# Score steps of two units regrouped: seven groups for two units instead of four for one, with PV in the spare PSUM banks

## The chip, the cores and the metric

One core of one Trainium2 chip. The metric is the device time of one execution in microseconds (us). The engines are TensorE (PE, with PEld for its weight loads), VectorE (DVE), ScalarE (ACT), GpSimd (POOL) and SyncE (SP, which here only issues DMAs).

## The reference, cut to what matters

```python
# q, k, v: (8, 12, 448, 64) float32
q_n, k_n = rmsnorm(q, g_q), rmsnorm(k, g_k)
scores = 1/sqrt(64) * q_n @ k_n.T
attn = exp(scores - max) / sum
x = (attn @ v) laid out as (3584, 768)
h = x @ w_in                      # 768 x 2048
out = maximum(0.01*h, h) @ w_out  # 2048 x 768
```

The kernel works in 24 units of four heads (three units to a batch). A unit needs scores in seven steps, exponentials, PV (attn @ v) and the sums z. Every exponential of a unit has one bias, called its shift: VectorE takes the maximum of the unit's step 0 (`shift_max`), a matmul spreads it over the partitions (`shift_mm`, tile `pb`), and VectorE reduces that to the bias `eb`. Until the shift is there, ScalarE can compute no exponential of the unit, and the scores stay in their slots. A slot is a pair of banks of PSUM, the memory that the matmuls here write. When a batch's three units are done, its dense layers go into a queue of items: 6 matmuls of layer 1 (`hps`), or 8 matmuls of layer 2 (`op`). The queue is fed out between the groups of score steps of later units, so that TensorE always has dense work while ScalarE computes exponentials.

## The kernel before

A score step is four matmuls on a quarter of the array each (64x64 tiling). Two score slots of two PSUM banks alternate; four more banks ("spare") serve everything else.

```python
    def slot():
        return psum.tile([P, 2, 512], FP32, tag="sT", bufs=2, name="sT")

    def aux(shape, dtype, name):
        return psum.tile(shape, dtype, tag="aux", bufs=4, name=name)

    def shift_mm(u):                       # after shift_max(u) on VectorE
        ...
        nc.tensor.matmul(pb[:, 0:P], onesp, s["dg"], start=True, stop=True)
        nc.vector.tensor_reduce(s["spare"][:, 510:511], pb[:, 0:P], axis=AXL.X, op=ALU.max)
        s["eb"] = ...                      # bias of every exponential of the unit
        nc.vector.tensor_scalar(s["eb"], s["spare"][:, 510:511], -1.0, DELTA, op0=ALU.mult, op1=ALU.add)

    def pv_slot(u):                        # PV takes a score slot
        s["pslot"] = slot()
        ...
    def pv_out(u):
        nc.scalar.copy(s["x32"], s["pslot"][:, :, 0:S])
    ...
    STEPS = ((0,), (1, 2), (3, 4), (5, 6))
    ...
        for u in range(3, NU):
            for d in range(4):             # four groups for each unit
                ...
                    qk(u, STEPS[d])
                    if d == 0:
                        shift_max(u)
                        if narrow(u - 1):
                            pv_slot(u - 1)
                            zcol(u - 1)
                            shift_mm(u)
                            pv_out(u - 1)
                            zcol_sum(u - 1)
                        ...
                    ex(u)                  # exponentials on ScalarE
                ...
                if d == 1 and u > 3 and narrow(u - 1):
                    xmul_pool(u - 1)       # x = PV * (1/z), on POOL
                ...
                fill(u, d, jobs)           # dense items, with small jobs between them
```

## Time and profile before

| | before |
|---|---|
| first three runs | 437.13 us (437.05 to 437.75) |
| profiled span | 435.7 us |
| TensorE busy | 419.9 us (96%) |
| ScalarE, VectorE busy | 309.9 us (71%), 215.6 us (49%) |
| TensorE waiting for another engine after 98 us | none listed |

TensorE is full, and after 98 us the profile puts nothing in its way. From there on a change pays only if it removes something from TensorE's own stream; whatever makes TensorE wait comes straight on top.

### The profile page before, as it was taken

Reading aid. Unit: us, or ns where it says so; the run is one execution under the profiler, and the core shown is the slowest. Engines: PE = TensorE matmul, PEld = TensorE weight load, DVE = VectorE, ACT = ScalarE, POOL = GpSimd, SP = SyncE. Lnnn points to the kernel's source line nnn. Section 1 sums busy time; section 2 is a strip of 40 time slices with the busy share of each in tenths; the row PEclk is TensorE's granted clock in tenths of the full one; section 3 lists DMA queues with packets and bytes.
Section 4 is the critical chain, followed back from the end, with each engine's and each line's share of the span. In section 5 each row is a group of like instructions: output and inputs, shape, how many; then the busy total and the mean of one; then the engine's idle time right before and its main releaser. Section 6 shows DMA issues by size and latency. Waiting matters only on the chain.

```text
span 435.7 us, 8818 instructions
## 1 busy us (share of the span) xinstructions
PE 419.9 (96%) x3714; PEld 216.9 (50%) x3714; DVE 215.6 (49%) x321; ACT 309.9 (71%) x460; POOL 148.8 (34%) x102
## 2 busy tenths in 40 slices
PE   6878999999999999999999999999999999999995
PEld 6645444444455544554445544554445544555563
DVE  4897565874535744554455745555356611220021
ACT  5989878688976699867876699867877486634300
POOL 4997565633422432532430423522521110100000
PEclk9899999999999999999999999999999999999999
DMA  7999995789458856669447875778524530311022
GB/s 262 248 259 255 238 235 76 195 195 201 96 144 145 215 152 119 136 200 201 91 126 141 200 186 98 154 205 165 125 45 100 132 84 2 78 38 38 0 73 73
DMA packets 66315, 62.37 MB, mean 143 GB/s; under 512 B 35684, under 2 KB 61284, under 8 KB 66276
## 3 DMA queue, kind: packets, MB, share of 16 engines
q1 hardware_dynamic: 55840, 49.82, 44.7%
q0 software_dynamic: 10272, 11.80, 17.4%
q8 instruction: 29, 0.48, 0.4%
q10 hardware_dynamic: 164, 0.20, 0.1%
q14 instruction: 10, 0.08, 0.1%
HBM read 45.61 MB, written 11.01 MB: 130 GB/s over the span
## 4 chain that ended last, share of the span: by engine, by line
PE 84%; ACT 7%; DVE 6%; DMA 2%; issue 1%; SPq 0%; DVEq 0%; ACTq 0%
PE hps L329 33%; PE op L351 31%; PE sT L179 8%; PE sT L314 5%; ACT et L198 3%; PE zc L260 3%; DVE n L151 1%; DMA rk<-in_k_dram 1%; PE pb L228 1%; DVE ssq L139 1%; PE sT L243 1%; PE pv L314 1%; ACT et L196 1%; DVE xt L323 1%; DMA out_dram<-ost 1%
## 5 line engine op out<-in xcount | busy, mean ns | idle before, releaser
L198 ACT ACTIVATE et<-sT,eb 128x896 f16<-128x896 f32 x166 | 158.7, 1004 | 48.0 <-PE sT L179 35.7
L351 PE MATMUL op<-wout,gt 128*128 128x384 f16 x896 | 153.6, 326 | 0.0
L329 PE MATMUL hps<-xt,win 128*128 128x448 f16 x756 | 151.0, 353 | 0.2 <-DVE xt L323 0.2
L351 PEld LDWEIGHTS <-gt 128*128 128x128 f16 x896 | 84.7, 98 | 65.3 <-issue 12.2
L329 PEld LDWEIGHTS <-win 128*128 128x128 f16 x756 | 70.9, 98 | 71.8 <-issue 7.6
L294 POOL TENSOR_TENSOR xt<-x,rz 128x896 f16<-128x896 f32 x19 | 40.9, 2154 | 185.6 <-DMA rz<-zs 170.7
L331 ACT ACTIVATE gt<-hps 128x448 f16<-128x448 f32 x126 | 67.6, 543 | 22.6 <-PE hps L329 21.5
L359 DVE COPY ost<-op 128x384 f32<-128x384 f32 x54 | 30.0, 556 | 94.2 <-PE op L351 90.9
L134 POOL TENSOR_TENSOR qg<-rq,ggb 128x896 f32<-128x896 f32 (+2 forms) x25 | 61.3, 2454 | 36.9 <-DVE n L151 32.6
L179 PE MATMUL sT<-qkT 64*64 64x448 f16 x664 | 52.3, 364 | 4.5 <-ACT et L198 3.8
L151 DVE TENSOR_TENSOR n<-qg,rinv 128x896 f16<-128x896 f32 (+2 forms) x25 | 27.1, 1085 | 54.5 <-POOL xt L294 23.6
L139 DVE TENSOR_REDUCE ssq<-sq 128x14 f32<-128x896 f32 (+2 forms) x49 | 50.0, 1054 | 1.9 <-ACT sq L126 1.9
L216 DVE TENSOR_REDUCE sT<-sT 128x1 f32<-128x896 f32 x22 | 24.1, 1094 | 30.6 <-PE sT L179 30.4
L151 DVE TENSOR_TENSOR n<-rk,rinv 128x896 f16<-128x896 f32 (+2 forms) x25 | 34.2, 1372 | 0.0
L179 PEld LDWEIGHTS <-qkT 64*64 64x64 f16 x672 | 15.2, 104 | 37.9 <-issue 35.4
L272 ACT COPY x<-sT 128x896 f32<-128x896 f32 x19 | 17.2, 905 | 18.0 <-PE sT L314 18.0
L314 PE MATMUL sT<-et,vt 64*64 64x448 f16 x532 | 28.4, 349 | 0.0
L314 PEld LDWEIGHTS <-vt 64*64 64x64 f16 x672 | 19.8, 107 | 10.5
L106 POOL DMA_DIRECT2D vt<-in_v_dram x24 | 18.3, 763 | 0.0
L126 ACT ACTIVATE sq<-rq 128x896 f32<-128x896 f32 (+2 forms) x19 | 17.3, 913 | 1.2 <-DMA rq<-in_q_dram 1.2
L126 ACT ACTIVATE sq<-rk 128x896 f32<-128x896 f32 x17 | 16.2, 955 | 0.7 <-DMA rk<-in_k_dram 0.7
L260 PE MATMUL zc<-et,onesr 128*32 128x448 f16 (+1 forms) x304 | 16.1, 332 | 0.0
(66 smaller groups left out, 216.3 us busy)
## 6 DMA issues: line engine op xcount, KB each, us to landing
rq<-in_q_dram SPq DMA_DIRECT2D x24, 448.0 KB, 4.6
rk<-in_k_dram SPq DMA_DIRECT2D x24, 448.0 KB, 6.1
out_dram<-ost SPq DMA_DIRECT2D x54, 192.0 KB, 3.5
rz<-zs SPq DMA_DIRECT2D x38, 224.0 KB, 3.5
vt<-in_v_dram POOLq DMA_DIRECT2D x24, 224.0 KB, 4.7
win<-in_moe_w_in_dram POOLq DMA_DIRECT2D x8, 384.0 KB, 11.5
wout<-in_moe_w_out_dram POOLq DMA_DIRECT2D x2, 1536.0 KB, 26.9
qkT<-n SPq DMA_TRANSPOSE x18, 4.1
```

The lines of the kernel that those rows point to most:

```text
L126: nc.scalar.activation(buf(u, "sq")[:, ti, :, c[0]:c[1]], raw[u][ti][:, :, c[0]:c[1]], AF.Square)
L134: eng.tensor_tensor(buf(u, "qg")[:, :, c[0]:c[1]], raw[u][0][:, :, c[0]:c[1]], ggb[:, None, None, :].broadcast_to([P, 2, n, D]), op=ALU.mult)
L139: nc.vector.tensor_reduce(buf(u, "ssq")[:, ti, :, c[0]:c[1]], buf(u, "sq")[:, ti, :, c[0]:c[1]], axis=AXL.X, op=ALU.add)
L151: nc.vector.tensor_tensor(buf(u, "n16")[:, ti, c[0]:c[1]].rearrange("p s a d -> p a s d"), src[:, :, c[0]:c[1]], buf(u, "rinv")[:, ti, :, ...
L179: nc.tensor.matmul(banks[a][64 * r:64 * r + 64, 0:S].rearrange("p (t x) -> p t x", t=NS), kT(u, r, a, t), qT(u, r, a), start=True, stop=True)
L198: nc.scalar.activation(s["et"][:, t], sT[:, :, 0:S], AF.Exp, bias=s["eb"], scale=1.0)
L294: nc.gpsimd.tensor_tensor(xts[b][:, g], s["x32"], s["rz"], op=ALU.mult)
L314: nc.tensor.matmul(s["pv"][r][64 * a:64 * a + 64, 0:S], vts[u % NV][64 * r:64 * r + 64, a, t], s["et"][64 * r:64 * r + 64, t, a], start=(t ...
L329: nc.tensor.matmul(hps[:, 0:S], win16[:, kt // 2, kt % 2, ts(ft, P)], xt[:, kt // 2, kt % 2], start=(kt == 0), stop=(kt == KT - 1))
L331: nc.scalar.activation(gt[:, ft, ds(S * (b % 2), S)], hps[:, 0:S], AF.Prelu, bias=0.0, scale=1.0, alpha=0.01)
L351: nc.tensor.matmul(op2[:, 0:HC], gt[:, ft, ts(t, P)], wout16[:, ft, ds(HC * half, HC)], start=(ft == 0), stop=(ft == FT - 1))
L359: nc.vector.tensor_copy(ost[0][:, ds(HC * half, HC)], op2[:, 0:HC])
```

## The change

The intent: fewer, fuller groups. Seven steps don't divide by two, so a unit had one group of one step and three of two. Two units have fourteen steps, seven groups of two (called x0 to x6 below). As x0 and x4 then use both slots for scores, PV moves to two spare banks. Also POOL's multiply for unit 4 is written behind the norms of unit 7. The diff, cut to its core:

```diff
     def pv_out(u):
-        nc.scalar.copy(s["x32"], s["pslot"][:, :, 0:S])
+        ...                                        # still so where PV has a slot
+        for r in range(2):
+            nc.scalar.copy(s["x32"][:, r], s["pv"][r][:, 0:S])
...
+    for u in range(PAIRS, NU, 2):                  # PAIRS = 8
+        order = [(u, t) for t in range(NS)] + [(u + 1, t) for t in range(NS)]
+        for x in range(NS):
+            groups.append((order[2 * x:2 * x + 2], (2.9, 4.0, 4.0, 4.0, 2.9, 4.0, 4.0)[x]))
...
+                elif d == 2:                       # units up to 7: four groups as before
+                    norms(u)
+                    if u == 5:
+                        job(xmul_pool, 4)          # was at d == 1
...
+            if x == 0:
+                shift_max(u)
+                pv(u - 1)                          # spare banks
+                zcol(u - 1)
+                shift_mm(u)
+                pv_out(u - 1)
+                ...
+            elif x == 3:                           # last step of u, step 0 of n = u + 1
+                ex(u)
+                shift_max(n)
+                job(lambda: None)                  # after the first dense item: nothing
+                job(shift_ex, n)                   # after the second: shift_mm(n), ex(n)
+            elif x == 4:                           # begins with steps 1 and 2 of n
+                pv(u)
+                zcol(u)
+                pv_out(u)
+                ...
```

More of the change, by code (lines that the diff above doesn't have):

```diff
@@ L43 @@
     NV = 5
+    PAIRS = 8
     cst = ctx.enter_context(tc.tile_pool(name="cst", bufs=1))
@@ L182, in qk @@
     def qk(u, steps):
-        st[u]["sT"] = []
+        st[u].setdefault("sT", [])
         for t in steps:
@@ L198, in ex @@
                 nc.scalar.activation(s["et"][:, t], sT[:, :, 0:S], AF.Exp, bias=s["eb"], scale=1.0)
+        s["sT"] = []
     def score0(u):
@@ L270, in pv_out @@
         s = st[u]
+        if "pslot" in s:
+            s["x32"] = zpool.tile([P, 2, S], FP32, tag="x32", name="x32")
+            nc.scalar.copy(s["x32"], s["pslot"][:, :, 0:S])
+            return
         s["x32"] = zpool.tile([P, 2, S], FP32, tag="x32", name="x32")
-        nc.scalar.copy(s["x32"], s["pslot"][:, :, 0:S])
+        for r in range(2):
+            nc.scalar.copy(s["x32"][:, r], s["pv"][r][:, 0:S])
     def zcol_sum(u):
@@ L379, in push_moe2, with fed, fill @@
                     queue.append((1.31, lambda b=b, t=t, half=half, part=part: moe2(b // 2, t, half, part)))
-    WD = (3.6, 2.9, 2.8, 2.8)
     STEPS = ((0,), (1, 2), (3, 4), (5, 6))
     debt = [0.0]
+    groups = [((), 3.6)] + [([(3, t) for t in STEPS[d]], 2.9) for d in range(1, 4)]
+    for u in range(4, PAIRS):
+        for d in range(4):
+            groups.append(([(u, t) for t in STEPS[d]], (3.6, 2.9, 2.8, 2.8)[d]))
+    FIRST = len(groups)
+    for u in range(PAIRS, NU, 2):
+        order = [(u, t) for t in range(NS)] + [(u + 1, t) for t in range(NS)]
+        for x in range(NS):
+            groups.append((order[2 * x:2 * x + 2], (2.9, 4.0, 4.0, 4.0, 2.9, 4.0, 4.0)[x]))
     def narrow(u):
         return 4 <= u < NU - 1
-    def fed(u, d):
-        return u % NQ == 0 and d == 3
-    def fill(u, d, jobs):
-        total = sum(c for c, _ in queue)
-        left = WD[d] + 3.0
-        uu, dd = u, d
-        while True:
-            dd += 1
-            if dd == 4:
-                uu, dd = uu + 1, 0
-            if uu == NU or (fed(uu, dd) and (u > 3 or uu > 3)):
+    def fed(gi):
+        if gi < FIRST:
+            u, d = 3 + gi // 4, gi % 4
+            return u // NQ if u > 3 and u % NQ == 0 and d == 3 else 0
+        y, x = divmod(gi - FIRST, NS)
+        u = PAIRS + 2 * y
+        if x == 3 and u % NQ == 0:
+            return u // NQ
+        if x == 0 and (u - 1) % NQ == 0:
+            return (u - 1) // NQ
+        return 0
+    def fill(gi, jobs):
+        total = sum(c for c, _ in queue)
+        w = groups[gi][1]
+        left = w + 3.0
+        for gj in range(gi + 1, len(groups)):
+            if fed(gj) > 0:
                 break
-            left += WD[dd]
-        debt[0] += total * WD[d] / left
+            left += groups[gj][1]
+        debt[0] += total * w / left
         while queue and debt[0] >= queue[0][0] * 0.5:
@@ L595, with early @@
         del queue[0:2]
-        for u in range(3, NU):
-            for d in range(4):
-                if d > 0 or u > 3:
-                    qk(u, STEPS[d])
-                    if d == 0:
-                        shift_max(u)
-                        if narrow(u - 1):
-                            pv_slot(u - 1)
-                            zcol(u - 1)
-                            shift_mm(u)
-                            pv_out(u - 1)
-                            zcol_sum(u - 1)
-                        else:
-                            zsum_slot(u - 1)
-                            pv(u - 1)
-                            shift_mm(u)
-                            zinv(u - 1)
+        def early(u):
+            if u + 4 < NU:
+                job(load, u + 4)
+            if u + 2 < NU:
+                prep_qg(u + 2, nc.gpsimd)
+            if u + 3 < NU:
+                load_v(u + 3)
+            if u < 6:
+                prep_sqp(u + 3)
@@ new lines, in sums_of_squares, with norms, squares @@
+        def sums_of_squares(u):
+            if u + 2 < NU:
+                for ti in range(2):
+                    job(prep_ssq, u + 2, ALL, (ti,))
+        def norms(u):
+            if u + 2 < NU:
+                job(prep_rinv, u + 2)
+                for ti in range(2):
+                    job(prep_norm, u + 2, ALL, (ti,))
+                if u > 3:
+                    job(prep_trd, u + 2)
+        def squares(u, ti):
+            if 6 <= u < NU - 3:
+                job(prep_sq, u + 3, ALL, (ti,))
@@ new lines, in shift_ex, with job @@
+        def shift_ex(u):
+            shift_mm(u)
+            ex(u)
+        for gi, (steps, w) in enumerate(groups):
+            jobs = []
+            def job(fn, *args):
+                jobs.append(lambda: fn(*args))
+            for u, t in steps:
+                qk(u, (t,))
+            if gi < FIRST:
+                u, d = 3 + gi // 4, gi % 4
+                if d == 0 and u > 3:
+                    shift_max(u)
+                    if narrow(u - 1):
+                        pv_slot(u - 1)
+                        zcol(u - 1)
+                        shift_mm(u)
+                        pv_out(u - 1)
+                        zcol_sum(u - 1)
+                    else:
+                        zsum_slot(u - 1)
+                        pv(u - 1)
+                        shift_mm(u)
+                        zinv(u - 1)
+                if gi > 0:
@@ L614 @@
                     ex(u)
-                jobs = []
-                def job(fn, *args):
-                    jobs.append(lambda: fn(*args))
                 if d == 0:
@@ L627 @@
                         xmul(u - 1)
-                    if u + 4 < NU:
-                        job(load, u + 4)
-                    if u + 2 < NU:
-                        prep_qg(u + 2, nc.gpsimd)
-                    if u + 3 < NU:
-                        load_v(u + 3)
-                    if u < 6:
-                        prep_sqp(u + 3)
-                if d == 1 and u > 3 and narrow(u - 1):
-                    xmul_pool(u - 1)
-                if fed(u, d) and u > 3:
-                    push_moe1(u // NQ - 1)
-                    push_moe2(u // NQ - 1)
@@ L641 @@
-                if (u, d) in ((3, 1), (4, 0)):
-                    for ti in range(2):
-                        prep_tr(u + 1, ti, VV)
-                if u + 2 < NU:
-                    if d == 1:
-                        for ti in range(2):
-                            job(prep_ssq, u + 2, ALL, (ti,))
-                    if d == 2:
-                        job(prep_rinv, u + 2)
-                        for ti in range(2):
-                            job(prep_norm, u + 2, ALL, (ti,))
-                        if u > 3:
-                            job(prep_trd, u + 2)
@@ L654 @@
-                if d == 3 and 6 <= u < NU - 3:
-                    for ti in range(2):
-                        job(prep_sq, u + 3, ALL, (ti,))
-                fill(u, d, jobs)
+                    early(u)
+                    if u == 4:
+                        for ti in range(2):
+                            prep_tr(5, ti, VV)
+                elif d == 1:
+                    if u > 3 and u != 5 and narrow(u - 1):
+                        xmul_pool(u - 1)
+                    if u == 3:
+                        for ti in range(2):
+                            prep_tr(4, ti, VV)
+                    sums_of_squares(u)
+                elif d == 2:
+                    norms(u)
+                    if u == 5:
+                        job(xmul_pool, 4)
+                else:
+                    for ti in range(2):
+                        squares(u, ti)
@@ new lines @@
+                if fed(gi) > 0:
+                    push_moe1(fed(gi) - 1)
+                    push_moe2(fed(gi) - 1)
+                fill(gi, jobs)
+                continue
+            y, x = divmod(gi - FIRST, NS)
+            u = PAIRS + 2 * y
+            n = u + 1
+            if x == 0:
+                shift_max(u)
+                pv(u - 1)
+                zcol(u - 1)
+                shift_mm(u)
+                pv_out(u - 1)
+                zcol_sum(u - 1)
+                ex(u)
+                job(zcol_inv, u - 1)
+                early(u)
+                sums_of_squares(u)
+            elif x == 1:
+                ex(u)
+                xmul_pool(u - 1)
+                norms(u)
+            elif x == 2:
+                ex(u)
+                for ti in range(2):
+                    squares(u, ti)
+            elif x == 3:
+                ex(u)
+                shift_max(n)
[5 more added lines that the diff above has]
+                pv_out(u)
+                zcol_sum(u)
+                ex(n)
+                job(zcol_inv, u)
+                early(n)
+                sums_of_squares(n)
+            elif x == 5:
+                ex(n)
+                xmul_pool(u)
+                norms(n)
+            else:
+                ex(n)
+                for ti in range(2):
+                    squares(n, ti)
@@ L658 @@
+            if fed(gi) > 0:
+                push_moe1(fed(gi) - 1)
+                push_moe2(fed(gi) - 1)
+            fill(gi, jobs)
         zsum_slot(NU - 1)
```

## The prediction

> **What bounds the kernel now.** I began with the busy shares, then asked who makes TensorE wait, then read the chain of waits over two units, then one timeline where a wait was left.
>
> ```profile
> PE 419.9 (96%) x3714; PEld 216.9 (50%) x3714; DVE 215.6 (49%) x321; ACT 309.9 (71%) x460; POOL 148.8 (34%) x102
> ...
> PE   6878999999999999999999999999999999999995
> ```
>
> This is the page: TensorE is busy in every slice from the seventh on. ACT averages 71%, and in the stretches that run the first dense layer (160 to 180 us) the windows by 20 us give it 19.0 of 20. The share proves nothing alone, as matmul ends are modelled, so I looked at TensorE's waits.
>
> ```profile
> PE sT L179 <- ACT et L198: 3.8, 9, 0.9
> PE pb L228 <- DVE dg L218: 1.8, 3, 0.8
> ```
>
> Columns: total us, times, longest. Asked by window, both rows are empty after 98 us. So from 98 to 430 us TensorE never waits for another engine; only fewer or cheaper matmul slots can shorten this stretch, and any new wait lengthens it. The chain over one unit shows what its slots cost:
>
> ```profile
> 198.21 4.54 PE hps L329 x24
> 202.75 0.50 PE sT L179 x8
> 203.25 2.38 PE hps L329 x12
> 205.63 0.50 PE sT L179 x8
> 206.13 3.51 PE hps L329 x18
> ...
> 213.65 0.31 PE sT L179 x4
> 213.97 1.32 PE sT L314 x28
> 215.29 0.78 PE zc L260 x16
> 216.07 0.16 PE pb L228
> 216.23 3.40 PE hps L329 x18
> ```
>
> Columns: start, us, what. 18 dense matmuls take 3.40 us when another full-array matmul precedes them (0.189 each) and 3.51 after a score group: 0.11 us for leaving the 64x64 tiling. 28 PV matmuls take 1.32 us, four at a time, so 8 scores should take 0.38 and take 0.50, and 4 should take 0.19 and take 0.31: 0.12 us for entering it. A score group thus costs 0.23 us beyond its work. This is the only waste in the chain that the change can reach after 98 us.
>
> The 0.8 us wait sits here:
>
> ```profile
> 80.52 1.09 DVE L151 TENSOR_TENSOR n<-qg,rinv 128x896 f16<-128x896 f32 x1
> 80.82 2.73 POOL L294 TENSOR_TENSOR xt<-x,rz 128x896 f16<-128x896 f32 x1 [3.95 <-DMA rz<-zs]
> 81.53 2.98 DVE L151 TENSOR_TENSOR n<-rk,rinv 128x896 f16<-128x896 f32 x1
> ...
> 84.90 1.08 DVE L216 TENSOR_REDUCE sT<-sT 128x1 f32<-128x896 f32 x1
> ...
> 86.35 0.22 PE L228 MATMUL pb<-dg,onesp 128*128 128x128 f16 x1 [0.84 <-DVE dg L218]
> ```
>
> In unit 5 the second norm takes 2.98 us where its neighbour takes 1.09, because POOL's multiply for unit 4 runs beside it; DVE then is late for unit 6's maximum and TensorE idles 0.84 us. The multiply itself started at 80.82 because its broadcast 1/z landed then.
>
> **What the Trainium skill says.** "TensorEngine Tiling (Array Packing)", Key Properties: changing the tiling mode drains TensorE. The chain agrees: 0.12 us in, 0.11 us out. "SBUF — State Buffer", Who interferes with whom: a VectorE instruction with two SBUF inputs contends with a GpSimd instruction that reads SBUF. The timeline agrees: 2.98 against 1.09 us. "PSUM — Partial Sum Buffer", Engine vs sequencer instructions: the queues of ScalarE, VectorE and GpSimd are strict FIFO. All my ordering arguments use it; the trace shows nothing against it.
>
> **The change part by part.** I compared the built instruction orders of the two programs.
>
> (1) The multiply moved behind the norms. On POOL the order is unchanged (squares of unit 8, multiply of unit 4, then the next q-times-g), and the multiply waits on the same semaphores with the same values: the two broadcasts and the copy of PV. Writing it later in the source adds no dependency on the norms. So it again starts when the broadcast lands, about 80.8 us, and collides again. Worth: 0; if it worked, 0.84 us.
>
> (2) Units 4 to 7: the same groups. The fill only moves one half-projection (8 matmuls) from group 4 to group 3 of unit 5 and shifts a few later; the TensorE total is equal. Worth: 0.
>
> (3) From unit 8 on, 16 units in 8 pairs. Before, a pair had 8 score groups: 2 of 0.31 and 6 of 0.50, 3.62 us; after, 7 of 0.50, 3.50: 0.12 saved. Returns from a score group straight to dense work: before 6 at 0.11; after 5, plus one from the z sums of the first unit (x4, below), which no longer has a shift matmul behind it. The shift matmuls cost 2 x 0.16 before; after, one 0.16, and one of about 0.05 amid dense matmuls (0.16 less the 0.11 switch). So 0.66 + 0.32 = 0.98 becomes 0.66 + 0.21 = 0.87: 0.11 saved. Together 0.23 per pair, x8 = **1.9 us saved**. PV, z sums and dense matmuls are unchanged in number.
>
> (4) The new wait. Call a pair's seven groups x0 to x6. x3 computes the first unit's last step and the second unit's step 0, then two dense items, the shift matmul, and the rest of its fill. x4 begins with steps 1 and 2 of the second unit. The two score slots alternate, so step 2 needs the slot of step 0, free only after shift, VectorE's bias and the exponential. Before, at a usual boundary: shift 250.15, reduce 250.42, bias 250.75, exponential 250.95 to 251.96. So 1.81 us from the shift's start, plus 0.05 to hand over (67.79 to 67.84 at an early wait) = 1.86. TensorE meanwhile has, by the built order:
> - pairs 8, 14, 20: shift 0.05 + 8 projections 1.30 + step 1 at 0.31 = 1.66; waits 0.2.
> - pairs 12, 18: 0.05 + 6 dense 1.13 + 0.31 = 1.49; waits 0.37. Here an output copy of 0.56 us comes just before the bias in VectorE's queue; I take it to start 0.1 after the shift's start, so the reduce starts near 0.65 instead of 0.27: 0.39 more, 0.76 in all.
> - pairs 10, 16, 22: two dense items, 2.3 us: no wait.
> Sum 3 x 0.2 + 2 x 0.76 = **2.1 us added**. TensorE has no slack elsewhere, so it goes straight into the span.
>
> (5) PV in the spare banks. At x0 two PV banks, the z bank and the shift bank take all four spare banks, so every activation of the group before must be done first; and dense work then waits for ACT to copy PV (now two copies instead of one of 0.91). A ledger for pair 12/14, where six groups of dense layer 1 follow each other, with starts read off ACT at 157 to 166 us (exponential 0.89, activation 0.42, square 0.84 from start to start): from the PV of x4 to the last activation ACT needs some 13.4 us and TensorE reaches the shift after 14.7. It fits by about 1.3 us. I allow **0.3 us** over all eight pairs for cases where it doesn't.
>
> Sum: 437.1 - 1.9 + 2.1 + 0.3 = 437.6. I take **437.4**, leaning a little to the gain, as each wait in (4) depends on tenths.
>
> **Rivals.** (a) The new slot waits do not come, because the profile's 1.81 us contains slack I can't see or ACT is early: then only the switches count, 435.2. For: TensorE never waited for a slot after 98 us before. Against: the slot chain is a plain dependency, and before step 0 had a slot of its own for 5 us. (b) The multiply does move behind the norms in time and the collision goes: another 0.8 less, 434.4 with (a). Against: same queue, same semaphores. (c) ACT becomes the bound in the dense-layer-1 stretches: 95% busy in 160 to 180 us, and PV copies, squares and activations now gate the same four banks. Three boundaries have squares between activations just ahead of PV (units 8, 14, 20); at 0.8 us each, 2.4 more, 440. Against: the ledger above.
>
> **Range and chances.** The best case (a with b) is 434.4, the worst I can build (4 plus c) is 440. The runs before spread over 0.7 us. Eight in ten: 434.6 to 439.6. Two per cent is 8.7 us, over four times the whole saving, and the waits would have to be four times my sum: faster 0.01, within 0.975, slower 0.015.
>
> **What would show it.** TensorE's busy share stays at 95 to 96%. The waits list gains a row of score matmuls waiting for the exponential after 98 us, about 5 times, 2 us in all, the longest near 0.8; in time, only at x4. Each score group stays at 0.50 us and there are 8 fewer of them. The norm of about 3 us at 81 us and the 0.84 us wait of the shift matmul remain. Copies of PV appear as 128x448, 32 of them from unit 7 on. I am wrong if dense matmuls wait for PV copies or activations for more than 1 us in sum, if the shift waits for a bank at units 8, 14 and 20, or if the norm at 81 us drops to about 1.1.

## The result, and the profile after

| | before | after |
|---|---|---|
| median (6 runs each) | 437.44 us (436.85 to 438.05) | 438.17 us (437.45 to 438.49) |
| ratio of fast runs | | 1.0014, 95% interval 1.0001 to 1.0027 |
| profiled span | 435.7 us | 436.4 us |

A ratio is the mean time of one kernel's fast runs over that of the other's in the same rounds, so not quite the ratio of the medians quoted. About 0.15% slower.

Whole times scatter by half a microsecond and more, so I also read stages from the chain of waits. Its PV rows mark the units; a unit's PV stands in the first group of the next unit. First of the kernel before (start, us, what); the marks chosen are the PV of units 4, 6 and 23:

```profile
70.91 1.32 PE sT L314 x28
...
97.94 1.32 PE sT L314 x28
...
387.06 1.32 PE pv L314 x28
```

The same marks of the changed kernel:

```profile
70.63 1.32 PE sT L321 x28
...
97.66 1.32 PE sT L321 x28
...
387.70 1.32 PE pv L321 x28
```

| stage | before | after |
|---|---|---|
| start to unit 4's PV | 70.91 | 70.63 |
| unit 4's PV to unit 6's (holds the moved multiply) | 27.03 | 27.03 |
| unit 6's PV to unit 23's (holds the pairs) | 289.12 | 290.04 |
| unit 23's PV to the end | 48.6 | 48.7 |

The stages do the same work in both kernels. The loss of 0.92 us lies in the stage with the pairs. The first stage varies from trace to trace of these kernels; in those of the experiments unit 4's PV starts between 70.25 and 71.85.

The page of the changed kernel shows as little as the one before. Its first row:

```profile
PE 418.7 (96%) x3714; PEld 218.9 (50%) x3714; DVE 216.5 (50%) x321; ACT 308.4 (71%) x476; POOL 150.7 (35%) x102
```

The list of TensorE's waits, asked from 130 to 430 us, where the kernel before has no row (total us, times, longest):

```profile
PE sT L180 <- ACT et L199: 1.3, 2, 0.6
```

And the chain at two boundaries between x3 and x4, pair 8 (units 8 and 9) and pair 12:

```profile
130.00 0.07 PE pb L230
...
130.09 0.31 DVE sT L231
...
130.68 1.01 ACT et L199
...
131.74 0.38 PE sT L180 x4
132.12 1.32 PE pv L321 x28
...
192.94 2.72 PE op L358 x16
...
195.68 0.56 DVE ost L366
196.24 0.22 DVE sT L231
...
196.73 1.01 ACT et L199
...
197.79 0.38 PE sT L180 x4
198.17 1.32 PE pv L321 x28
```

The chain leaves TensorE here: shift matmul, VectorE's reduce and bias, ScalarE's exponential, and only then the second score step (0.38 us). In pair 12 an output copy (`ost`) stands before the reduce. Without the wait, PV of pair 8 would follow the end of its 16 projections at 130.00 by 0.06 (shift) + 1.30 (8 projections) + 0.50 (two score steps), at 131.86; it started at 132.12: 0.26 us lost. Pair 12, whose projections end at 192.94 + 2.72 = 195.66: 195.66 + 0.06 + 1.13 + 0.50 = 197.35 against 198.17: 0.82 us. The wait list shows only the two long ones (pairs 12 and 18). The short ones hide in the busy time: the eight score matmuls of pair 8 are one row of 0.83 us in the timeline instead of 0.57. (One step alone is a row of 0.38 us and two are 0.57, so a step without a wait starts 0.19 us before the one ahead of it ends. Only what a wait takes beyond this overlap is idle time: 0.64 of the 0.82 us in pair 12.)

### The profile page after: what moved, and what is told of

Read it like the earlier page. It is cut to its first block, busy times and chain, and to the rows that moved or that the text cites. A ratio compares the mean times of both kernels' runs of the same rounds, so it can differ in the third digit from the quotient of the medians.

```text
span 436.4 us, 8841 instructions
## 1 busy us (share of the span) xinstructions
PE 418.7 (96%) x3714; PEld 218.9 (50%) x3714; DVE 216.5 (50%) x321; ACT 308.4 (71%) x476; POOL 150.7 (35%) x102
## 4 chain that ended last, share of the span: by engine, by line
PE 82%; ACT 8%; DVE 6%; DMA 2%; issue 1%; SPq 0%; ACTq 0%; DVEq 0%
PE hps L336 33%; PE op L358 30%; PE sT L180 8%; PE pv L321 5%; ACT et L199 5%; PE zc L262 3%; DMA rq<-in_q_dram 2%; DVE n L152 1%; PE pb L230 1%; DVE ssq L140 1%; PE sT L245 1%; PE sT L321 1%; DVE sT L231 1%; ACT et L197 1%; DVE xt L330 1%
## 5 line engine op out<-in xcount | busy, mean ns | idle before, releaser
L301 POOL TENSOR_TENSOR xt<-x,rz 128x896 f16<-128x896 f32 x19 | 47.8, 2516 | 206.9 <-DMA rz<-zs 176.7
L135 POOL TENSOR_TENSOR qg<-rq,ggb 128x896 f32<-128x896 f32 (+2 forms) x25 | 56.7, 2271 | 15.7 <-DVE n L152 11.4
L152 DVE TENSOR_TENSOR n<-rk,rinv 128x896 f16<-128x896 f32 (+2 forms) x25 | 35.6, 1425 | 0.0
L279 ACT COPY x<-pv 128x448 f32<-128x448 f32 x32 | 15.5, 535 | 26.0 <-PE pv L321 26.0
L321 PE MATMUL pv<-et,vt 64*64 64x448 f16 x588 | 32.1, 349 | 0.0
L321 PEld LDWEIGHTS <-vt 64*64 64x64 f16 x672 | 20.9, 107 | 10.7 <-issue 0.4
L284 DVE COPY zs<-zc 64x448 f32<-64x448 f32 x19 | 11.9, 627 | 27.9 <-PE zc L262 27.5
```

The costliest lines, as they stand in the source:

```text
L135: eng.tensor_tensor(buf(u, "qg")[:, :, c[0]:c[1]], raw[u][0][:, :, c[0]:c[1]], ggb[:, None, None, :].broadcast_to([P, 2, n, D]), op=ALU.mult)
L152: nc.vector.tensor_tensor(buf(u, "n16")[:, ti, c[0]:c[1]].rearrange("p s a d -> p a s d"), src[:, :, c[0]:c[1]], buf(u, "rinv")[:, ti, :, ...
L301: nc.gpsimd.tensor_tensor(xts[b][:, g], s["x32"], s["rz"], op=ALU.mult)
L321: nc.tensor.matmul(s["pv"][r][64 * a:64 * a + 64, 0:S], vts[u % NV][64 * r:64 * r + 64, a, t], s["et"][64 * r:64 * r + 64, t, a], start=(t ...
```

## The experiments

The theory: the regrouping saves 0.23 us in each pair as TensorE changes its tiling less often, and this is more than given back in x4, where the second unit's step 2 waits for the slot of step 0, whose exponential hangs on a late shift. Rivals: PV in the spare banks costs the time (its two copies, and four banks that must all be free); the saving isn't real; the multiply matters.

| run | edit | us, median | before, same rounds | ratio (95%) | PV 4 to PV 6 | PV 6 to PV 23 |
|---|---|---|---|---|---|---|
| changed kernel | | 438.17 | 437.44 | 1.0014 (1.0001 to 1.0027) | 27.03 | 290.04 |
| e1_pv_between | PV between x4's steps | 436.12 | 437.48 | 0.9965 (0.9951 to 0.9980) | 27.03 | 287.57 |
| e6_shift_later | shift one item later | 446.05 | 437.26 | 1.0196 (1.0177 to 1.0214) | 27.02 | 297.60 |
| e9_shift_earlier | shift one item earlier | 438.72 | 437.14 | 1.0040 (1.0027 to 1.0054) | 27.02 | 290.92 |
| e5_split_groups | 16 more groups | 441.78 | 437.26 | 1.0099 (1.0084 to 1.0114) | 27.02 | 293.61 |
| e2_pv_banks_alone | before, PV in spare banks | 437.35 | 437.48 | 0.9996 (0.9981 to 1.0011) | 27.04 | 289.11 |
| e3_gate_multiply | multiply gated | 437.40 | 437.48 | 1.0000 (0.9987 to 1.0013) | 26.42 | 290.04 |
| e7_before_gated | before, multiply gated | 436.10 | 437.26 | 0.9972 (0.9959 to 0.9986) | 26.14 | 289.11 |
| e4_both | e1 and e3 | 435.90 | 437.48 | 0.9965 (0.9952 to 0.9979) | 26.43 | 287.57 |
| e8_both_pairs_from_6 | e4, pairs from unit 6 | 435.70 | 437.14 | 0.9966 (0.9954 to 0.9979) | other work | other work |

All results were correct. The last two columns come from each run's chain, as above. They repeat to 0.02 us where nothing was edited, so they show parts that the medians cannot.

**e1: take the wait away, and nothing else.** PV needs no new score, so it can stand between step 1 and step 2, in the same tiling; step 2 is then issued 1.32 us later.

```diff
-            for u, t in steps:
+            for u, t in (steps[:1] if x4 else steps):
                 qk(u, (t,))
...
                 pv(u)
+                qk(n, (steps[1][1],))
                 zcol(u)
```

> The changed kernel with one reordering: in group x4 the second unit's step 2 is issued after the first unit's PV instead of before it, in the same tiling mode. My theory (the saving of 1.8 us in tiling switches is real, and eaten by score step 2 waiting for the slot of step 0): all five waits in x4 vanish, 2.4 us less than the changed kernel, some 435.7 us, and 1.5 us under the kernel before (ratio about 0.996). Rival 1 (the PV copies and the four gated banks eat the saving): no change, 438.2. Rival 2 (no saving exists, the difference is noise): within 0.5 us of both.

The chain of this run at the boundary of pair 12:

```profile
195.82 1.14 PE hps L336 x6
196.96 0.31 PE sT L180 x4
197.27 1.32 PE pv L321 x28
198.59 0.19 PE sT L180 x4
198.78 0.78 PE zc L262 x16
```

TensorE never leaves its own rows, and the step behind PV costs its bare 0.19 us. The stage falls by 2.47 us, and is now 1.55 us shorter than before the change. My theory said 2.4 and 1.5. Rival "banks" expected no change and falls: PV is still in the spare banks here.

**e6 and e9: move the shift.** One more dummy job ahead of the shift makes the wait longer; one fewer makes the shift itself come early.

```diff
                 job(lambda: None)
+                job(lambda: None)                  # e6
                 job(shift_ex, n)
```

```diff
-                job(lambda: None)                  # e9
                 job(shift_ex, n)
```

> The changed kernel with the second unit's shift matmul one dense item later in x3. My theory (what ends the wait in x4 is the chain shift, reduce, bias, exponential of 1.86 us, less the dense work after the shift): waits of about 1.9 us in pairs 8, 14 and 20 (an output copy then stands before the reduce), 1.5 in pairs 12 and 18, 0.4 in pairs 10, 16 and 22: 9.8 in sum against 2.4, so 6 to 8 us more, 444 to 446. Rival (the slot is not what is waited for): no change beyond 1 us.

> The changed kernel with the second unit's shift matmul one dense item earlier in x3, the other way to free the slot in time. My theory: the slot waits go (2.5 us), but now the shift comes before VectorE's maximum is ready, about 2.2 us after the group's start (score 0.5, hand-over 0.2, maximum 1.1, diagonal 0.3), and TensorE reaches it after 1.9 us in five pairs and 1.75 in three: new waits of 5 x 0.3 + 3 x 0.45 = 2.8 us, so within 0.5 us of the changed kernel, 438.2 to 438.7. Rival (the place of the shift is simply wrong, and earlier is free): 435.7, like PV between the steps.

The timeline of e6, first score wait of pairs 8, 10 and 12 (start, us, engine, line, operation, then the idle time before it and who ended it):

```profile
133.99 0.38 PE L180 MATMUL sT<-qkT 64*64 64x448 f16 x4 [1.78 <-ACT et L199]
167.46 0.38 PE L180 MATMUL sT<-qkT 64*64 64x448 f16 x4 [0.18 <-ACT et L199]
201.08 0.38 PE L180 MATMUL sT<-qkT 64*64 64x448 f16 x4 [1.31 <-ACT et L199]
```

All eight pairs wait now, with the sizes in the expected order (1.9, 0.4, 1.5 were expected), and the stage grows by 7.56 us. So the slot is what is waited for. In e9 the score waits are gone and the shift waits instead, for VectorE's maximum, in all eight pairs; the one of pair 8 in its timeline:

```profile
128.50 0.22 PE L230 MATMUL pb<-dg,onesp 128*128 128x128 f16 x1 [0.19 <-DVE dg L220]
```

The listed waits sum to 2.0 us (0.19 in five pairs, 0.36 in three). The stage is 290.92 - 287.57 = 3.35 us longer than in e1, which has neither wait (2.8 was expected). Pair by pair, between the PV rows of x0 and x4, it is 0.35 us in pairs such as 8 (18.60 in e9 against 18.06 in e1, less the step of 0.19 that e1 has behind PV) and 0.53 in pairs such as 10 (19.30 against 18.58, less 0.19): 5 x 0.35 + 3 x 0.53 = 3.34. So here too the list states each wait some 0.16 us short. Moving the shift trades one wait for another; moving PV removes it.

**e5: is the saving real?** The score steps of x1 and x5 are split by a dense item: the same matmuls, sixteen more groups.

```diff
+            if part:                               # x1 and x5
+                def second(u=steps[1][0], t=steps[1][1]):
+                    qk(u, (t,))
+                    ex(u)
+                job(second)
```

> The changed kernel with groups x1 and x5 each split in two: the second score step goes after the first dense item. Same matmuls, 16 more entries into and returns from the 64x64 tiling. My theory (a group costs 0.23 us beyond its work): 16 x 0.23 = 3.7 us more than the changed kernel, some 441.9. Rival (the switch is an artefact of modelled matmul ends, or hidden): less than 1 us more.

The chain of this run in x1 of pair 10:

```profile
151.92 0.31 PE sT L180 x4
152.23 1.24 PE hps L336 x6
153.47 0.31 PE sT L180 x4
153.78 2.38 PE hps L336 x12
```

Each single step costs 0.31 us, not 0.19, and each return to dense work 0.11. The stage grows by 3.57 us, 0.223 for each group: from PV row to PV row it is 0.22 to 0.24 for fifteen of them, and 0.12 for x1 of pair 8, where the changed kernel loses 0.13 us (told below) and this one does not. So a group's cost is real time, not an artefact of modelled ends.

**e2: the banks alone.** The kernel before, with only PV moved to spare banks:

```diff
-                            pv_slot(u - 1)
+                            pv(u - 1)
...
-        nc.scalar.copy(s["x32"], s["pslot"][:, :, 0:S])
+        for r in range(2):
+            nc.scalar.copy(s["x32"][:, r], s["pv"][r][:, 0:S])
```

> The kernel before with only PV moved to two spare banks and its copy split in two, four groups per unit throughout. My theory: the banks cost nearly nothing, 0 to 0.5 us over the kernel before (ratio 1.000 to 1.001). Rival 1 (the banks and copies eat the saving): 2 us or more, ratio 1.005, with dense matmuls or the shift matmul waiting for ACT.

289.11 against 289.12 us: in this grouping the banks cost nothing that can be measured.

**e3 and e7: the multiply.** Moving the line did nothing to POOL's order. Here a one-column copy on POOL that reads unit 7's second norm is put before the multiply, in the changed kernel (e3) and, with the move, in the kernel before (e7).

```diff
                     if u == 5:
+                        job(gate, 7)               # POOL reads the norm
                         job(xmul_pool, 4)
```

> The changed kernel with a one-column POOL copy that reads unit 7's second norm put before unit 4's multiply, so that the multiply does wait for the norms. My theory (moving the line in the source had no effect because POOL's order and waits stayed): now the norm at 81 us takes 1.1 us instead of 2.97, the 0.55 us wait of the shift matmul goes, 0.4 to 0.6 us less than the changed kernel. Rival (the move already did what it could, or the wait has another cause): no change.

> The kernel before with only the multiply of unit 4 gated on unit 7's norms. My theory: the 0.84 us wait at 86 us goes and nothing else changes, 0.5 to 0.9 us less than the kernel before, ratio 0.998 to 0.999. Rival (the wait at 86 us is made up for later): no change.

The timeline of the changed kernel, with the move but without the gate:

```profile
80.24 1.09 DVE L152 TENSOR_TENSOR n<-qg,rinv 128x896 f16<-128x896 f32 x1
80.54 2.73 POOL L301 TENSOR_TENSOR xt<-x,rz 128x896 f16<-128x896 f32 x1 [3.95 <-DMA rz<-zs]
81.25 2.97 DVE L152 TENSOR_TENSOR n<-rk,rinv 128x896 f16<-128x896 f32 x1
...
86.08 0.22 PE L230 MATMUL pb<-dg,onesp 128*128 128x128 f16 x1 [0.55 <-DVE dg L220]
```

And of e3:

```profile
80.89 1.08 DVE L152 TENSOR_TENSOR n<-rk,rinv 128x896 f16<-128x896 f32 x1
82.04 0.19 POOL L236 COPY gate_t<-n 128x1 f16<-128x1 f16 x1 [5.80 <-DVE n L152]
82.17 2.08 POOL L301 TENSOR_TENSOR xt<-x,rz 128x896 f16<-128x896 f32 x1
```

In the changed kernel the multiply still starts 0.3 us after the first norm and the second norm still takes 2.97 us. With the gate the norm takes 1.08 us, the multiply 2.08 instead of 2.73, and the shift matmul waits no more. (Both engines lose by the overlap, and seem to take turns: in the changed kernel the multiply starts 0.79 us before the first norm ends and takes 0.65 longer than with the gate, the second norm starts 2.02 us before the multiply ends and takes 1.89 longer, and POOL's next product, `qg`, starts 0.98 us before that norm ends and takes 2.94 us instead of 2.09.) The stage from unit 4's PV to unit 6's falls by 0.61 us in e3 and by 0.89 in e7. (The wait was 0.84 before and 0.55 after, though the stage was equal: after, a changed fill put one projection item before unit 5's last score group, so unit 5's PV came 0.29 us later, behind unit 5's last exponential. That part the gate does not remove.)

**e4 and e8: what beats both kernels.** e4 has both edits. e8 sets `PAIRS = 6` in addition.

> The changed kernel with both edits: PV between the two score steps of x4, and the gated multiply. My theory: the two add, 2.4 + 0.5 = 2.9 us less than the changed kernel, some 435.2 us, ratio to the kernel before about 0.995. Rival 1: no more than the gate's 0.5.

> The best version so far (PV between the score steps, gated multiply) with the paired groups from unit 6 on, nine pairs instead of eight. My theory (a pair saves 0.2 us of tiling switches and nothing else is at stake): 0.2 us less than with eight pairs, 435.7, ratio to the kernel before 0.996; the difference can be read only in the trace, from unit 5's PV to the final z sums. Rival (a change this early moves the feeds of the first dense layer into waits): equal or slower.

In e4 the two parts add exactly in the trace: 26.43 and 287.57, 3.07 us less than the changed kernel in the two stages. The medians show 2.27, and only 0.22 between e1 and e4, where the trace shows 0.60; that is within the scatter of the runs (435.3 to 436.5 for both). For e8 the early fill differs, so I compare from unit 3's PV to unit 23's: 327.86 us in e8, 327.49 in e4. So the ninth pair did not pay, against my 0.2 us: with less fill early on, unit 4's PV waits 0.52 us for an exponential, and a score step in unit 6 for 0.15, which more than takes the gain. The rival was right. e4 is the better of the two by this stretch of the trace and e8 equal to it by the clock; both beat the kernel before by about 0.35%, and the changed kernel by about 0.5%.

## Why the prediction was right or wrong

- **The time.** 437.4 us was forecast, 438.17 measured, in the range. Against the kernel before I expected +0.3 and the medians say +0.7; the kernel before itself moved from 437.13 to 437.44 with three more runs. The last step, "leaning a little to the gain", was the wrong way.
- **The saving, 1.9 us.** Right. e1 has the saving without the waits and gains 1.55 us, and its chain shows two small losses beside it: 0.13 us in x1 of pair 8 (two score steps in 0.63 us instead of 0.50, waiting for the exponentials of x0), and 0.16 us in x0 of pair 10 (16 projections in 2.76 instead of 2.60). 1.55 + 0.29 = 1.84.
- **The new wait, 2.1 us.** Right in place, cause and pairs; a little small. 290.04 - 287.57 = 2.47 us measured, 0.26 in three pairs (0.2 forecast) and 0.82 in two (0.76 forecast): 3 x 0.26 + 2 x 0.82 = 2.42. The small part missed is in the chain: from the start of the shift to that of step 2 the timeline has 1.90 us in pair 8 (129.84 to 131.74; 1.86 forecast) and 2.31 in pair 12 (195.48 to 197.79; 2.25 forecast). Rival (a), no slot waits, is out.
- **The banks, 0.3 us.** The size came true (0.29, as just told) partly by luck: the first of its two parts, 0.13, is a wait for a score slot and not for a bank of PV (ScalarE sat idle for 0.45 us just before those exponentials, waiting for their shift). The second, 0.16, looks like the forecast wait for the copy of PV, though no run tests it: in pair 10 ScalarE's first copy starts at 148.14, 0.37 us after PV's last matmul ends (0.09 in pair 16, which loses nothing), takes some 0.53 us, and the projections start at 148.72, 0.05 after its end. Why that copy starts late stays open. e2 shows that the move of PV by itself costs nothing. Rival (c), ScalarE as the bound by way of the banks, did not happen.
- **The multiply, 0.** Right: the stage is 27.03 us in both kernels, and the norm still takes 2.97 us. The worth of a move that works was put at 0.84 us: e7 measured 0.89 in the kernel before, e3 0.61 in the changed one.
- **Units 4 to 7, 0.** Right in the sum, wrong in detail: the fill's change moved 0.29 us from the shift's wait to PV's. So the forecast "the 0.84 us wait remains" failed (0.55).
- **Rival (b)**, the multiply moves in time, did not happen either.
- **Slips without consequence.** TensorE's row of slices is at 9 from the fifth on, not the seventh, and at 5 in the last. For "slower" the waits would have had to be some five times the sum forecast (10.3 us against 2.1), not four.
- **The waits list.** I expected about five rows' worth, 2 us. It has two of 0.64, as waits of some 0.25 us show only as longer busy rows. The chain shows all five.

## What to carry to other kernels

When one engine is full, count what its own stream wastes and what new dependency each reordering puts before it, with the built order at hand; a saving of some tenths in each round is lost to a single chain of shift, reduce and exponential that is cut too short. If a wait appears, look first for work without that dependency that can stand in front of it in the same mode (PV here), before moving the producer, which may have its own producer just behind. Moving a line of source did not order the two engines here; a data dependency did.

## What the Trainium skill lacked or had wrong

- "TensorEngine Tiling (Array Packing)", Key Properties, says that a change of tiling mode drains TensorE but gives no cost. Here, between 64x64 and full-array matmuls of 448 columns: 0.12 us in and 0.11 us out by the chain, 0.223 us for each added group by e5.
- No page I looked up says that a short wait of TensorE may be missing from a list of waits: 0.26 us in pair 8 showed only as eight matmuls of 0.83 us in one row instead of 0.57, and in pair 12 the list has 0.64 of 0.82 us.
